# Forty more empty weight loads ahead of layer A's segments, and one more transposition ahead of the last outputs

## The chip, the cores and the metric

The kernel runs on one core of a Trainium2 chip. The metric is the device time of one execution in microseconds (us). The engines are named as in the profile: PE is TensorE's matrix multiplication and PEld its loading of weights, DVE is VectorE, ACT is ScalarE, POOL is GpSimd, SP is SyncE, which issues most of the DMA transfers.

## The reference

Four layers, A, B, A, B, each added to its input after a layer normalisation. Layer B is a linear attention and is not touched by the change. Layer A is recurrent: 2048 rows of 640 are cut into 64 segments of 32, and each segment is processed together with 8 memory rows that are the first outputs of the segment before.

```python
mem = mem0
for s in range(n_seg):                        # 64 segments of 32 rows
    xs = x[:, s * seg_len:(s + 1) * seg_len, :]
    h = jnp.concatenate([mem, xs], axis=1)    # 8 + 32 rows of 640
    q = jnp.einsum('btd,dhe->bhte', h, Wq)    # 32 heads of 192
    k = jnp.einsum('btd,dhe->bhte', h, Wk)
    v = jnp.einsum('btd,dhe->bhte', h, Wv)
    scores = jnp.einsum('bhqe,bhke->bhqk', q, k) * scale
    p = _softmax(jnp.where(mask[None, None], scores, -1000000000.0), axis=-1)
    o = jnp.einsum('bhqk,bhke->bhqe', p, v)
    o = jnp.einsum('bhte,hed->btd', o, Wo)
    mem = o[:, :M, :]                         # the next segment waits for this
    outs.append(o[:, M:, :])
```

## The kernel before

`A_pre` first does what does not depend on the memory: the keys, queries and values of the last 8 rows of every segment. `A_chain` then walks through the 64 segments in order. In it everything is in the order of the program text (`tc.manual_schedule()`): each engine executes its instructions in the order in which the Python code issues them, and semaphores make them wait for each other.

A segment has four rounds of eight heads. Per round TensorE projects queries, keys and values (`project`, line 1023, 20 matmuls each: five blocks of 128 input features in four column groups), computes scores (`scores`, lines 1060 and 1065), the sums of the exponentials (`sums`, line 1143, three matmuls), the weighted values (`attend`, line 1073, eight matmuls), and the round's share of the output product (`wo_round`, line 1102, 48 matmuls) into one PSUM tile `W` (`ps_w`). ACT and DVE turn one into the other: `normalise` takes logarithm and exponential of the sums on ACT (lines 1148 and 1149) and multiplies E on DVE (line 1150); `attend` ends with a copy of one half of OT on ACT (line 1079) and of the other on DVE (line 1080).

The end of a segment is the part that the change touches. There TensorE runs, in this order: the attention of round 2; `wo_round` of round 1, its last 24 matmuls around the three sums of round 3; 48 matmuls of `wo_round` of round 2 (whose OT lies in the tile `KT`); one matmul that only keeps TensorE busy (line 1109); `attend` of round 3; another such matmul; `wo_round` of round 3; four more busy matmuls (line 1116) and `fill(SEG_FILL)`, two weight loads of a single column (line 1122). DVE then transposes `W` (lines 1267 and 1268) into the first 8 columns of each 32-column block of `hT`, and the next segment's first projection waits for that.

The other columns of the next `hT` come from the next segment's rows, which have been loaded from DRAM long before (`load_rows`, POOL, line 974). `hx_transpose` (line 978) transposes them on DVE, in four instructions of 160 columns each. One of the four is issued between `normalise` of round 3 and the copies at the end of its `attend`; the other three come after these copies. `load_rows` for the segment after the next one is issued behind the fourth, since it overwrites the rows.

`fill(n)` issues n weight loads of one column, which compute nothing. `FILL` gives their number once per layer A, in its first segment, behind the first query projection:

```python
to_rows(q_or_k("Q", 0), "Q")
if s == 0:
    fill(FILL[li])
to_rows(q_or_k("K", 0), "K")
```

A segment has 510 matmuls, each with its weight load, and the two loads of `fill(SEG_FILL)`: 1022 TensorE instructions. The trace shows two semaphore instructions more on TensorE's queue in each segment, which makes 1024.

SP's queue carries the weights that don't fit into SBUF: per segment the slots of wQ, wK and wV (`load_slots`, line 694) near its beginning, and the output weights of the last round (`load_wo`, line 726, three transfers called wo_rows) near its middle. POOL's queue carries the small transfers: kqb (line 994), vb (line 1006), otb (line 1093).

Of the kernel before, what the change touches and what calls it, by code (L numbers as in the profile page):

```python
# [17 lines left out]
SLOTS = {"Q": 3, "K": 3, "V": 3}  # L18
LN_EPS = 1e-5

FILL = {0: 78, 2: 79}
SEG_FILL = 2

LATE = 64512
# [91 lines left out]
class Kernel:  # L116
# [834 lines left out]
    def A_chain(self, xn_dram, at_dram, li, load_slot, piece, load_wo, late_wo, wo_mid, wo_end, low, copy_slots):  # L951
# [3 lines left out]
        with tc.tile_pool(name=f"A{li}_ch", reuse_waits="tile", bufs=1) as sp, \  # L955
# [17 lines left out]
            def load_rows(s):  # L973
                nc.gpsimd.dma_start(out=xr[8:32, :], in_=xn_dram[32 * s:32 * s + 24, :])

            def hx_transpose(hT, gs):
                for g in gs:
                    nc.vector.transpose(out=hT[32 * g:32 * g + 32, :, :],
                                        in_=xr[:, 160 * g:160 * g + 160].rearrange("p (j b) -> p b j", b=KC))

            def new_hT():
                return sp.tile([P, KC, 32], BF16, name="hT", tag="hT")
# [53 lines left out]
            def to_rows(raw, m):  # L1036
                if m == "K":
                    nc.vector.transpose(out=KT[:, :, 0:64], in_=raw[:, :].rearrange("p (c j) -> p c j", j=64))  # L1038
                else:
                    rv = raw[:, :].rearrange("p (x i j) -> p x i j", i=3, j=64)  # L1040
                    nc.vector.transpose(out=QT[:, :, 0:4:3, 0:64], in_=rv[:, :, 0:3:2, :])  # L1041
                    nc.vector.transpose(out=QT[0:64, :, 1, 0:64], in_=rv[0:64, :, 1, :])
                    nc.vector.transpose(out=QT[64:P, :, 2, 0:64], in_=rv[64:P, :, 1, :])  # L1043
# [53 lines left out]
            def wo_round(W, r, OT, first, last, part=range(12)):  # L1097
                w = low[:, 0:7680] if last_wo == r else wo_end[:, :] if r in (0, 3) else wo_mid[:, 7680 * (r - 1):7680 * r]
                for i in part:
                    c, q = i % 6, 32 * (i // 6)  # L1100
                    for g in range(4):
                        nc.tensor.matmul(W[32 * g:32 * g + 32, 0:160], lhsT=OT[:, c, q:q + 32],  # L1102
                                         rhs=w[:, 640 * i + 160 * g:640 * i + 160 * g + 160], start=(first and i == 0),
                                         stop=(last and i == 11), tile_position=(0, 32 * g), skip_group_check=True)
# [14 lines left out]
            def fill(n):  # L1119

                for _ in range(n):
                    nc.tensor.ldweights(self.ident[:, 0:1])  # L1122
# [39 lines left out]
            hT = new_hT()  # L1162
# [3 lines left out]
            for s in range(NSEG):  # L1166
# [6 lines left out]
                def q_or_k(m, n):  # L1173
                    ps = pqp.tile([P, 512], F32, name="ps_qk", tag="qk")
                    project(hT, ps, m, n, s, range(KC))
                    return to_raw(ps, "OT" if m == "K" and n == 0 else "raw")
# [11 lines left out]
# [3 lines that stand above are left out]
# [54 lines left out]
                normalise(S, E)  # L1245
                if s + 1 < NSEG:
                    hT = new_hT()
                    hx_transpose(hT, range(1))
                wo_round(W, order[L - 1], OT, False, False)
                idle = pqp.tile([P, 512], F32, name="ps_idle", tag="qk")  # L1250
                keep_busy(idle, 1, 384)
# [2 lines left out]
                if s == NSEG - 1:  # L1254
                    self.first_tails = tails, [self.spread_tails(0, tails[0], low, "vvss")]
                if s + 1 < NSEG:
                    hx_transpose(hT, range(1, 4))
                    if s + 2 < NSEG:
                        load_rows(s + 2)
                keep_busy(idle, 1, 512)  # L1260
# [91 lines left out]
```

## Time and profile before

| | us |
|---|---|
| median of 3 runs | 3619.94 |
| the runs | 3619.16, 3619.94, 3630.49 |
| the profiled execution | 3620.12 |
| its span in the trace | 3618.4 |
| PE busy | 3296.9 (91%) |
| DVE busy | 2331.4 (64%) |
| ACT busy | 2028.7 (56%) |
| 64 segments of the first layer A | 204.3 to 1551.6 |
| 64 segments of the second | 2019.7 to 3367.0 |

A segment takes 1347.3 / 64 = 21.05 us on average, and the 128 of them are 74% of the span. The granted TensorE clock is 1.00 in both stretches, so the times of the trace need no correction for it. "Busy" of PE includes modelled ends of pipelined matmuls. In rows of waits, "issue" is time in which an engine waited for nothing that the profile shows.

### The profile page before, as it was taken

To read this page: it belongs to the slowest core of one execution; us is meant where nothing else is said; L and a number is where in the kernel's file an instruction comes from. 1 tells how busy PE (TensorE), PEld (TensorE's weight loads), DVE (VectorE), ACT (ScalarE), POOL (GpSimd) and SP (SyncE) were. 2 spreads that over 40 slices of the span, in tenths; PEclk is the share of its full clock that TensorE was granted. 3 is DMA by queue.
4 is the path that set the end of the run, shared out by engine and by line. 5 is a ranking of instruction groups with operands and counts; after the bars stand their busy time and mean duration, and the time that the engine had idled before them with its cause. 6 is when DMAs were issued, how large, how long until landed. Compare 5 with 4: busy or idle time off the path is not lost.

```text
span 3618.4 us, 166133 instructions
## 1 busy us (share of the span) xinstructions
PE 3296.9 (91%) x70978; PEld 2277.0 (63%) x71391; DVE 2331.4 (64%) x6320; ACT 2028.7 (56%) x5233; POOL 1596.8 (44%) x4173
## 2 busy tenths in 40 slices
PE   9989898998999989889999889899999899998999
PEld 7756666666666666655377566666666666666553
DVE  5456666766666766646633566666666666666465
ACT  3356565666566656546433556665666566665463
POOL 3445555555555555430123455555545555554400
PEclk9999999999999999999999999999999999999999
DMA  8888877777777777760476777777777777777600
GB/s 321 327 314 315 308 290 271 294 290 283 269 292 283 293 269 285 284 222 1 145 276 214 287 269 284 288 291 274 286 295 285 273 276 292 290 280 272 233 1 30
DMA packets 261055, 936.23 MB, mean 259 GB/s; under 512 B 53962, under 2 KB 104026, under 8 KB 226778
## 3 DMA queue, kind: packets, MB, share of 16 engines
q1 hardware_dynamic: 190650, 824.56, 60.0%
q0 software_dynamic: 67744, 87.80, 7.8%
q8 instruction: 557, 9.13, 1.0%
q10 hardware_dynamic: 1920, 13.24, 0.9%
q14 instruction: 184, 1.51, 0.1%
HBM read 855.58 MB, written 80.81 MB: 259 GB/s over the span
## 4 chain that ended last, share of the span: by engine, by line
PE 57%; DVE 12%; ACT 10%; issue 9%; DMA 6%; PEld 4%; POOL 1%; SPq 1%; ACTq 0%; DVEq 0%; POOLq 0%
PE ps_qk L1023 15%; PE ps_w L1102 9%; PE ps_v L1023 6%; PE ps_o L1073 5%; PE ps_pre L913 4%; PE ps_s L1065 4%; DVE E L1150 3%; ACT raw L1033 3%; DVE QT L1041 3%; ACT ps_s L1149 3%; PEld L1102 3%; ACT ps_s L1148 2%; DVE QT L1043 2%; PE ps_pre L937 2%; PE ps_s L1060 2%
## 5 line engine op out<-in xcount | busy, mean ns | idle before, releaser
L1023 PEld LDWEIGHTS <-hT 128*32 128x32 bf16 x30720 | 873.7, 96 | 435.5 <-DVE hT L1268 73.2
L1023 PE MATMUL ps_qk<-arena,hT 128*32 128x384 bf16 x20480 | 1043.0, 328 | 87.0 <-DVE hT L1268 75.1
L1033 ACT ACTIVATE raw<-ps_qk 128x384 bf16<-128x384 f32 x1024 | 502.9, 491 | 380.6 <-DVE QT L1043 251.9
L1023 PE MATMUL ps_v<-arena,hT 128*32 128x384 bf16 x10240 | 594.1, 326 | 9.0 <-DMA arena<-wV 5.4
L1006 POOL DMA_DIRECT2D Vp<-vb x512 | 259.2, 506 | 631.3 <-PE ps_o L1073 589.5
L1102 PE MATMUL ps_w<-arena,OT 128*32 128x160 bf16 x18432 | 466.8, 234 | 12.2 <-DMA arena<-wo_rows 4.8
L1102 PEld LDWEIGHTS <-OT 128*32 128x32 bf16 x18432 | 389.9, 97 | 75.4 <-ACT OT L1079 46.1
L1038 DVE STREAM_TRANSPOSE KT<-raw 128x384 bf16<-128x384 bf16 x512 | 296.2, 579 | 193.6 <-ACT raw L1033 189.7
L1041 DVE STREAM_TRANSPOSE QT<-raw 128x256 bf16<-128x256 bf16 x512 | 228.1, 445 | 239.6 <-ACT raw L1033 195.9
L994 POOL DMA_DIRECT2D kqb<-kqb x512 | 292.1, 571 | 169.1 <-POOL KT L1002 147.0
L1093 POOL DMA_DIRECT2D otb<-otb x512 | 283.9, 554 | 116.7 <-DVE otb L1089 88.6
L1054 DVE CAST Vp<-ps_v 64x384 bf16<-64x384 f32 x512 | 286.2, 559 | 69.6 <-ACT Vp L1052 57.4
L1150 DVE TENSOR_TENSOR E<-E,ps_s 80x320 bf16<-80x320 bf16 x512 | 247.1, 483 | 113.7 <-ACT ps_s L1149 113.3
L1073 PEld LDWEIGHTS <-Vp 80*128 80x128 bf16 x4096 | 200.5, 99 | 152.2 <-issue 137.6
L1052 ACT ACTIVATE Vp<-ps_v 64x384 bf16<-64x384 f32 x512 | 244.9, 478 | 90.2 <-PE ps_v L1023 90.1
L1073 PE MATMUL ps_o<-E,Vp 80*128 80x80 bf16 x4096 | 233.9, 202 | 62.9 <-DVE E L1150 43.2
L986 ACT ACTIVATE Vp<-ps_w 32x160 bf16<-32x160 f32 x512 | 150.7, 294 | 232.8 <-PE L1122 175.2
L1127 ACT ACTIVATE E<-ps_s 80x320 bf16<-80x320 f32 x512 | 221.8, 433 | 76.4 <-PE ps_s L1065 36.4
L1079 ACT ACTIVATE OT<-ps_o 128x192 bf16<-128x192 f32 x384 | 126.3, 329 | 246.0 <-PE ps_o L1073 230.8
L1102 PE MATMUL ps_w<-arena,KT 128*32 128x160 bf16 x6144 | 162.9, 238 | 106.4 <-issue 106.3
L1080 DVE CAST OT<-ps_o 128x192 bf16<-128x192 f32 x384 | 137.5, 358 | 161.6 <-PE ps_o L1073 152.0
L999 POOL COPY QT<-kqb 128x64 bf16<-128x64 bf16 x512 | 125.4, 245 | 251.4 <-PE ps_s L1065 247.7
(158 smaller groups left out, 5514.4 us busy)
## 6 DMA issues: line engine op xcount, KB each, us to landing
arena<-wK SPq DMA_DIRECT2D x121, 1152.0 KB, 7.7
arena<-wV SPq DMA_DIRECT2D x117, 1152.0 KB, 10.3
arena<-wo_rows SPq DMA_DIRECT2D x128, 960.0 KB, 6.2
arena<-wQ SPq DMA_DIRECT2D x125, 768.0 KB, 5.6
arena<-wo_rows SPq DMA_DIRECT2D x128, 640.0 KB, 7.8
arena<-wQ SPq DMA_DIRECT2D x125, 384.0 KB, 3.9
arena<-wo_rows SPq DMA_DIRECT2D x140, 320.0 KB, 8.1
arena<-in_A_Wv_dram SPq DMA_DIRECT2D x76, 384.0 KB, 8.6
```

The costliest lines, as they stand in the source:

```text
L994: nc.gpsimd.dma_start(out=kqb[:], in_=self.kqb_d[r, :, s, :])
L1006: nc.gpsimd.dma_start(out=Vs[n % 2][64:80, :], in_=self.vb_d[s, r].rearrange("g t f -> (g t) f"))
L1023: nc.tensor.matmul(o[32 * g:32 * g + 32, 0:384], lhsT=hT[:, b, :], rhs=rhs, start=(i == 0), stop=(i == KC - 1), tile_position=(0, 32 * g), ...
L1033: nc.scalar.activation(out=raw[:], in_=ps[:, 0:384], func=ACT.Copy)
L1038: nc.vector.transpose(out=KT[:, :, 0:64], in_=raw[:, :].rearrange("p (c j) -> p c j", j=64))
L1041: nc.vector.transpose(out=QT[:, :, 0:4:3, 0:64], in_=rv[:, :, 0:3:2, :])
L1052: nc.scalar.activation(out=o, in_=i, func=ACT.Copy)
L1054: nc.vector.tensor_copy(out=o, in_=i)
L1073: nc.tensor.matmul(O[x][:, 80 * i:80 * i + 80], lhsT=Vs[n % 2][0:80, 448 * x + k:448 * x + k + 128], rhs=E[0:80, 160 * x + 80 * e:160 * x ...
L1093: nc.gpsimd.dma_start(out=self.otb_d[:, s, 96 * r:96 * r + 96], in_=otb[:, :, :].rearrange("p c t -> p (c t)"))
L1102: nc.tensor.matmul(W[32 * g:32 * g + 32, 0:160], lhsT=OT[:, c, q:q + 32], rhs=w[:, 640 * i + 160 * g:640 * i + 160 * g + 160], start=(firs ...
L1150: nc.vector.tensor_tensor(out=E[0:80, 0:320], in0=E[0:80, 0:320], in1=rc, op=ALU.mult)
```

## The change

`FILL[0]` goes from 78 to 118: forty more one-column weight loads in the first segment of the first layer A. As TensorE has a single stream of instructions, everything behind them stands 40 places later in it, in that layer and in all that follow, the second layer A with its unchanged 79 included. And `hx_transpose` does two of its four transpositions, not one, between `normalise` of round 3 and the copies of `attend`; two are left behind these copies.

```diff
-FILL = {0: 78, 2: 79}
+FILL = {0: 118, 2: 79}
...
                 normalise(S, E)
                 if s + 1 < NSEG:
                     hT = new_hT()
-                    hx_transpose(hT, range(1))
+                    hx_transpose(hT, range(2))
                 wo_round(W, order[L - 1], OT, False, False)
                 idle = pqp.tile([P, 512], F32, name="ps_idle", tag="qk")
                 keep_busy(idle, 1, 384)
...
                 if s + 1 < NSEG:
-                    hx_transpose(hT, range(1, 4))
+                    hx_transpose(hT, range(2, 4))
                     if s + 2 < NSEG:
                         load_rows(s + 2)
                 keep_busy(idle, 1, 512)
```

The order of every engine's instructions is otherwise the same in both kernels.

## The prediction

> **What bounds the kernel now.** I read first the page's busy times, then the waits of PE, then the timeline of one ordinary segment's end, then the DMA view in narrow windows. The page:
>
> ```profile
> PE 3296.9 (91%) x70978; PEld 2277.0 (63%) x71391; DVE 2331.4 (64%) x6320; ACT 2028.7 (56%) x5233; POOL 1596.8 (44%) x4173
> ...
> q8 instruction: 557, 9.13, 1.0%
> ```
>
> PE is the bound on average, but look at the instruction queue: 557 packets, 9.13 MB, so 16.4 KB each. PE and PEld have 70978 + 71391 = 142369 instructions, 255.6 per packet: TensorE's program arrives in blocks of 256. A segment of 1024 instructions is four blocks exactly, so the borders fall on the same four places of every segment.
>
> The waits of PE (line waited for, us in total, times, longest):
>
> ```profile
> PE ps_w L1102 <- issue: 106.3, 119, 2.3
> PE ps_qk L1023 <- DVE hT L1268: 75.1, 126, 0.7
> PE ps_o L1073 <- DVE E L1150: 43.2, 129, 0.9
> ```
>
> The largest has no releaser: 119 times, 0.89 us each, nearly once per segment. The timeline of the segment that runs from 2659.66 to 2680.83 shows where (start, duration, engine, line):
>
> ```profile
> 2675.49 0.10 PEld L1143 LDWEIGHTS <-ones_blk 80*32 80x32 bf16 x3
> 2675.50 0.44 PEld L1102 LDWEIGHTS <-OT 128*32 128x32 bf16 x16
> ...
> 2675.90 0.10 PEld L1102 LDWEIGHTS <-KT 128*32 128x32 bf16 x1
> 2675.91 0.41 ACT L1148 ACTIVATE ps_s<-ps_s 80x320 f32<-80x320 f32 x1 [0.21 <-PE ps_s L1143]
> ...
> 2676.35 0.41 ACT L1149 ACTIVATE ps_s<-ps_s 80x320 f32<-80x320 f32 x1
> ...
> 2677.16 1.01 PE L1102 MATMUL ps_w<-arena,KT 128*32 128x160 bf16 x47 [0.95 <-issue]
> ...
> 2677.38 0.47 DVE L1150 TENSOR_TENSOR E<-E,ps_s 80x320 bf16<-80x320 bf16 x1
> ...
> 2678.27 0.45 PE L1073 MATMUL ps_o<-E,Vp 80*128 80x80 bf16 x8
> ...
> 2678.76 0.36 DVE L1080 CAST OT<-ps_o 128x192 bf16<-128x192 f32 x1 [0.53 <-PE ps_o L1073]
> ...
> 2679.00 1.01 PE L1102 MATMUL ps_w<-arena,OT 128*32 128x160 bf16 x48
> ...
> 2679.15 1.10 DVE L978 STREAM_TRANSPOSE hT<-Vp 32x160 bf16<-32x160 bf16 x3
> ...
> 2680.29 0.28 DVE L1267 STREAM_TRANSPOSE wt<-ps_w 128x96 f32<-128x96 f32 x1
> ```
>
> The first KT matmul runs at once, the other 47 of the same group wait until 2677.16: a block border, with the next block not there. Meanwhile ACT and DVE do the normalisation, whose sums went out just before. The DMA view shows the segment's four instruction packets begin near 2660.87, 2668.38, 2674.84 and 2678.26. The third is the block that PE waits for; from its start to PE's restart are 2.32 us.
>
> **The border, 40 places earlier.** Counting back from the second KT pair: one KT pair, 16 OT pairs, 3 sum pairs, 20 pairs, 40 instructions. The new border lies exactly ahead of the three sums. PE reaches it at 2675.49; call the time at which the block is there R. The wait now delays the sums, so normalisation comes after it and not beside it. From the first sum's weights to the end of the multiplication: ACT ends at 2676.76, DVE adds 0.03 + 0.47, so 2677.26 - 2675.49 = R + 1.77 (here the multiplication came later, 2677.38, behind two otb copies). PE needs less for the 64 matmuls between (0.41 + 0.94) and the busy one (0.17), R + 1.52, so `attend` waits for E: R + 1.81.
>
> **The transposition moved** (344 to 393 ns each in the row of line 978) is worth something where it was: the three end at 2680.25, 0.04 before line 1267, while PE's last `wo_round` is over at 2679.00 + 1.01 = 2680.01. One fewer there would give 0.24. But ahead of the copy it has room only while E is early (multiplication over at 2677.85, copy at 2678.76). With `attend` right behind E, two transpositions end at +0.76 after the multiplication, the outputs are ready at +0.52, so the copy waits 0.25: starts at +0.78, ends at +1.14; from its end to line 1267 goes by PE, 2680.01 - 2679.12 + 0.03 = 0.92. Line 1267 starts at R + 1.77 + 2.06 = R + 3.83. Before it was 2680.29: break-even is R = 2676.46. POOL's `load_rows` stays behind the fourth transposition.
>
> **R.** The third fetch follows the entry into the block before. The old border there is 128 pairs ahead of the KT one, reached near 2670.75; the new one is 20 pairs of line 1023 earlier, 0.81 us, 2669.94. Bounds: the delay to the packet stays (4.1 us), R = 2677.16 - 0.81 = 2676.35, 0.11 gained; the packet starts when it did, R = 2677.16, 0.70 lost. What decides is the DMA traffic, and POOL's transfers show how it treats a request (KB, us from issue to landing; issued at 2665.12, 2667.53, 2669.31, 2669.88, 2671.88):
>
> ```profile
> kqb<-kqb POOLq DMA_DIRECT2D x1, 48.0 KB, 6.8
> ...
> Vp<-vb POOLq DMA_DIRECT2D x1, 28.0 KB, 5.5
> ...
> kqb<-kqb POOLq DMA_DIRECT2D x1, 48.0 KB, 5.3
> ...
> otb<-otb POOLq DMA_DIRECT2D x1, 24.0 KB, 7.2
> ...
> Vp<-vb POOLq DMA_DIRECT2D x1, 28.0 KB, 5.7
> ```
>
> They land at 2671.9, 2673.0, 2674.6, 2677.1, 2677.6. The first two: issued 2.41 apart, landed 1.1 apart, 0.46 us per us. The last two: 2.0 apart, landed 0.5 apart; behind SP's wo_rows (issued 2669.20 to 2670.48) asking earlier brings little. The second fetch is also just in time: 2668.38 + 2.32 = 2670.70 against PE at 2670.75. Asked 0.81 earlier it comes 0.37 earlier by the first slope, so PE stands 0.44 at the second border, and the third request is 0.37 early, not 0.81. With an unchanged delay from there, R = 2677.16 - 0.37 = 2676.79, which I take: it lies between the bounds and nearer to neither. Cost: 2676.79 + 3.83 - 2680.29 = 0.33 us per segment. The stand at the second border costs nothing of its own, being shorter than the wait that follows.
>
> The fourth fetch follows R, the border it serves lies in the last busy matmuls, and PE waits 0.60 for hT there: covered. The forty weight loads: 78 took 1.01 us at the first segment, so 0.52 once. In layer B and `A_pre` the waits of PE show no such entry: nothing.
>
> **Sum** against the profiled execution, 3620.12 us (0.18 from the median): 126 x 0.33 + 0.5 = 42, so 3662, rounded to 3660. About 0.3%, 11 us, is what a measurement here can tell from no change.
>
> [...]
>
> **Rivals.**
> - The borders' places don't matter, only the transposition does: the wait keeps its effect and 0.24 x 126 = 30 us are gained, 3590. Against it: what the wait covers changes. 0.06.
> - The third fetch gets ahead of the wo_rows traffic: with the second fetch's delay (2665.98 to 2668.38, 2.4) it starts at 2672.3, the block is there before 2675.49, and E bounds: multiplication over at 2677.85 (otb copies), line 1267 at 2679.91, 0.38 gained, more where otb is early. Partly so, R = 2676.1, 0.36. Some 45 to 75 us, 3575 to 3545. For it: 2669.94 lies before SP's last wo_rows issue. 0.20.
> - R within 0.09 of break-even, no change: 3620. 0.12.
> - The packet keeps its place behind wo_rows: 0.70 x 126 = 88, 3708. For it: otb, issued 2669.88, lands with those issued 2 us later. 0.20.
> - My forecast, R from 2676.55 to 2677.0: 11 to 70 us slower. 0.42.
>
> **Numbers.** Faster 0.06 + 0.20, same 0.12, slower 0.42 + 0.20. The range reaches from 3575, which leaves out the farther half of the fast case, to 3715, past the full loss. The forecast's own range is 3631 to 3690.
>
> **What would show it.** Right: the PE wait on "issue" leaves line 1102 and stands ahead of line 1143, ending near 1.3 us; PE line 1073 waits longer for line 1150; line 1080 starts some 0.25 after its outputs; 3 becomes 2 in the last row of line 978; a wait in a projection near 2669.9 of this segment. Wrong: no wait ahead of line 1143, the third instruction packet more than 1.2 us earlier in its segment, or a time under 3609.

## The result, and the profile after

| | before | after |
|---|---|---|
| median, us | 3619.55 (4 runs, 3615.25 to 3630.49) | 3709.04 (4 runs, 3701.61 to 3717.83) |
| profiled execution, us | 3620.12 | 3701.61 |
| ratio | | 1.0243, interval 1.0212 to 1.0275 |

The change costs 89 us. The direction and most of the mechanism are those of the forecast; the amount is near that of the rival "the packet keeps its place behind wo_rows" (3708), though not from its sum alone, as the last part of the account shows.

The page of the changed kernel:

```profile
PE 3369.9 (91%) x70978; PEld 2269.3 (61%) x71431; DVE 2334.3 (63%) x6320; ACT 2030.6 (55%) x5233; POOL 1590.2 (43%) x4173
...
q8 instruction: 557, 9.13, 1.0%
```

There are 40 more weight loads (71431 against 71391), as many instruction packets, and no more work on DVE and ACT. PE's 73 us more of "busy" come with the same 70978 matmuls: their ends are modelled, and it is no more work. The waits of PE (line waited for, us in total, times, longest):

```profile
PE ps_s L1143 <- issue: 60.2, 43, 2.0
PE ps_s L1143 <- ACT KT L1079: 50.1, 74, 1.1
PE ps_o L1073 <- DVE E L1150: 42.8, 129, 0.7
PE ps_qk L1023 <- DVE hT L1268: 31.6, 100, 0.4
PE ps_v L1023 <- issue: 22.7, 47, 1.0
PE ps_v L1023 <- DMA arena<-wV: 14.8, 16, 5.3
PE ps_idle L1116 <- issue: 13.0, 13, 2.8
```

The largest entry of before, 106.3 us at line 1102, is gone. In its place stand 60.2 + 50.1 = 110.3 us ahead of the sums of line 1143. The second of the two names ACT, whose copy to KT had ended 1.1 us before the wait was over (below), so it is read as the block border as well. Of the 43 + 74 waits, 59 lie in the first layer A and 58 in the second: the forty loads of the first moved the border in both. "PE ps_v L1023 <- issue" is new: the stand at the second border.

The timeline of an ordinary segment of the second layer A, from 3273.65 to 3295.54 (start, duration, engine, line):

```profile
3284.38 0.77 PEld L1023 LDWEIGHTS <-hT 128*32 128x32 bf16 x22 [0.41 <-issue]
...
3289.71 0.33 ACT L1079 ACTIVATE KT<-ps_o 128x192 bf16<-128x192 f32 x1
...
3291.11 0.10 PEld L1143 LDWEIGHTS <-ones_blk 80*32 80x32 bf16 x3 [1.25 <-issue]
...
3291.47 0.41 ACT L1148 ACTIVATE ps_s<-ps_s 80x320 f32<-80x320 f32 x1 [1.44 <-PE ps_s L1143]
...
3291.91 0.41 ACT L1149 ACTIVATE ps_s<-ps_s 80x320 f32<-80x320 f32 x1
3292.35 0.48 DVE L1150 TENSOR_TENSOR E<-E,ps_s 80x320 bf16<-80x320 bf16 x1 [1.04 <-ACT ps_s L1149]
...
3292.86 0.71 DVE L978 STREAM_TRANSPOSE hT<-Vp 32x160 bf16<-32x160 bf16 x2
3292.89 0.45 PE L1073 MATMUL ps_o<-E,Vp 80*128 80x80 bf16 x8
...
3293.61 0.36 DVE L1080 CAST OT<-ps_o 128x192 bf16<-128x192 f32 x1
...
3294.88 0.28 DVE L1267 STREAM_TRANSPOSE wt<-ps_w 128x96 f32<-128x96 f32 x1
```

Read it from the row of 3291.11: PE has stood 1.25 us and sends the first weights of the sums when the block is there. ACT has waited 1.44 us for the sums, DVE 1.04 for ACT. Before, this time lay beside the normalisation; now the normalisation comes after it. `attend` starts as soon as E is multiplied (3292.83), and the copy of line 1080 stands behind two transpositions, 0.72 after `attend` starts and not 0.49.

Where single segments scatter, medians tell more. All medians below are over the 126 ordinary segments of a run (all but the first of each layer A), worked out from the trace's records, in us from a segment's first instruction. The borders follow from counting off 256 instructions: a segment has 1024, and in the median four packets start in it, before and after. "Needed" is when PE's last instruction ahead of the border starts, "there" when the first one behind it does.

| | before | after |
|---|---|---|
| second block needed, there | 11.19, 11.28 | 10.38, 10.73 |
| third packet starts | 15.12 | 15.02 |
| third block needed, there (R) | 16.42, 17.54 | 16.18, 17.45 |
| multiplication over (L1150) | 17.88 | 19.18 |
| `attend` starts (L1073) | 18.66 | 19.24 |
| line 1267 starts | 20.68 | 21.28 |

PE gets to the third border 0.24 earlier and is let through 0.09 earlier, yet E is ready 1.30 later. Some of that was slack: before, `attend` came 0.78 after E. So line 1267 is 0.60 later, 126 x 0.60 = 76 us. PE's wait for wV was this before:

```profile
PE ps_v L1023 <- DMA arena<-wV: 5.4, 2, 4.6
```

It is 14.8 now, 9 more, and the 118 empty loads take 1.84 us where the 78 took 1.01, 0.8 more: 86, where the profiled executions differ by 81.5.

### The profile page after: what moved, and what is told of

It reads as the page before. It is cut to its first block, busy times and chain, and to the rows that moved or that the text cites. A ratio compares the mean times of both kernels' runs of the same rounds, so it can differ in the third digit from the quotient of the medians.

```text
span 3699.9 us, 166173 instructions
## 1 busy us (share of the span) xinstructions
PE 3369.9 (91%) x70978; PEld 2269.3 (61%) x71431; DVE 2334.3 (63%) x6320; ACT 2030.6 (55%) x5233; POOL 1590.2 (43%) x4173
## 3 DMA queue, kind: packets, MB, share of 16 engines
q10 hardware_dynamic: 1920, 13.24, 0.9%
## 4 chain that ended last, share of the span: by engine, by line
PE 54%; DMA 12%; DVE 12%; ACT 11%; issue 9%; PEld 1%; POOL 1%; SPq 1%; ACTq 0%; DVEq 0%; POOLq 0%
PE ps_qk L1023 14%; PE ps_w L1102 8%; PE ps_v L1023 7%; DMA arena<-wV 6%; PE ps_o L1073 5%; PE ps_pre L913 4%; DVE E L1150 4%; ACT ps_s L1149 3%; PE ps_s L1065 3%; ACT ps_s L1148 3%; ACT raw L1033 3%; DVE QT L1041 2%; PE ps_pre L937 2%; PE ps_s L1060 2%; DVE QT L1043 2%
## 5 line engine op out<-in xcount | busy, mean ns | idle before, releaser
L1023 PEld LDWEIGHTS <-hT 128*32 128x32 bf16 x30720 | 861.1, 97 | 446.4 <-issue 93.9
L1023 PE MATMUL ps_qk<-arena,hT 128*32 128x384 bf16 x20480 | 1031.8, 328 | 40.7 <-DVE hT L1268 31.6
L1023 PE MATMUL ps_v<-arena,hT 128*32 128x384 bf16 x10240 | 626.0, 327 | 44.1 <-issue 22.7
L1102 PE MATMUL ps_w<-arena,OT 128*32 128x160 bf16 x18432 | 508.8, 235 | 14.4 <-DMA arena<-wo_rows 5.1
L1150 DVE TENSOR_TENSOR E<-E,ps_s 80x320 bf16<-80x320 bf16 x512 | 247.3, 483 | 212.9 <-ACT ps_s L1149 212.6
L1073 PEld LDWEIGHTS <-Vp 80*128 80x128 bf16 x4096 | 199.4, 99 | 186.5 <-issue 178.5
L1148 ACT ACTIVATE ps_s<-ps_s 80x320 f32<-80x320 f32 x512 | 214.7, 419 | 157.5 <-PE ps_s L1143 157.5
L1073 PE MATMUL ps_o<-E,Vp 80*128 80x80 bf16 x4096 | 233.8, 202 | 69.6 <-DVE E L1150 42.8
L1143 PE MATMUL ps_s<-E,ones_blk 80*32 80x320 bf16 (+1 forms) x1536 | 159.5, 305 | 110.3 <-issue 60.2
L1065 PE MATMUL ps_s<-QT,KT 128*80 128x80 bf16 (+1 forms) x3072 | 233.1, 213 | 2.0 <-POOL KT L1002 1.8
```

The lines of the kernel that those rows point to most:

```text
L1023: nc.tensor.matmul(o[32 * g:32 * g + 32, 0:384], lhsT=hT[:, b, :], rhs=rhs, start=(i == 0), stop=(i == KC - 1), tile_position=(0, 32 * g), ...
L1065: nc.tensor.matmul(S[0:80, c0:c0 + 80 * (q1 - q0)], lhsT=KT[:, 3 * x + i, :], rhs=QT[:, x, q0:q1, :], start=False, stop=(x == 1 and i == 2 ...
L1073: nc.tensor.matmul(O[x][:, 80 * i:80 * i + 80], lhsT=Vs[n % 2][0:80, 448 * x + k:448 * x + k + 128], rhs=E[0:80, 160 * x + 80 * e:160 * x ...
L1148: nc.scalar.activation(out=rc, in_=rc, func=ACT.Ln)
L1150: nc.vector.tensor_tensor(out=E[0:80, 0:320], in0=E[0:80, 0:320], in1=rc, op=ALU.mult)
```

## The experiments

Ratios are against the kernel before on the same chip.

**One part at a time.** First the border alone:

```diff
-FILL = {0: 78, 2: 79}
+FILL = {0: 118, 2: 79}
```

> Only the forty weight loads, one transposition ahead of the copies as before. Theory (the block border ahead of the sums, its block arriving when the wo_rows traffic lets it, makes the whole loss): with `attend` right behind the multiplication the copy isn't held up, but three transpositions follow it, which gives R + 3.82 for line 1267 against R + 3.83 with two; so 3709 us within 6, and the wait ahead of line 1143 as in the changed kernel. Rival (the second transposition holds up the copy and that is a good part of the loss): under 3690.

Measured: 3727.21 us (3717.47 to 3752.52), ratio 1.0285, 1.0229 to 1.034. That is 3723 us by the 3619.55 of before, above the 3709 within 6 that was expected. Then the transposition alone:

```diff
-                    hx_transpose(hT, range(1))
+                    hx_transpose(hT, range(2))
...
-                    hx_transpose(hT, range(1, 4))
+                    hx_transpose(hT, range(2, 4))
```

> Only the second transposition moved, the borders where they were. Theory: where the border stands behind the sums, the multiplication is over 0.9 us before the copy, so two transpositions have room, and the end of the chain on DVE comes 0.24 us earlier in 126 segments: 3620 - 30 = 3590 us. Rival (the moved transposition delays the copy of OT in any case, or PE's last product is the later one): 3620 or above.

Measured: 3604.94 us (3595.78 to 3606.54), ratio 0.9939, 0.9909 to 0.9968, some 22 us of the 30 that were expected. The waits of PE with the border alone, then with the transposition alone:

```profile
PE ps_s L1143 <- issue: 66.9, 49, 2.2
PE ps_s L1143 <- ACT KT L1079: 45.9, 70, 1.2
```

```profile
PE ps_w L1102 <- issue: 108.2, 121, 2.0
PE ps_qk L1023 <- DVE hT L1268: 48.5, 126, 0.4
```

The border alone makes the wait at line 1143 (112.8 us) and the whole loss, by the ratios a little more, though the two intervals overlap. The transposition alone gains 0.6%: line 1267 starts at 20.51 and not 20.68, 0.17 x 126 = 21 us, and PE's wait for `hT` falls from 75.1 to 48.5. The two ratios multiply to 1.0222, within the interval of both together.

**Is it the border's place, or the moved fetches?** The changed kernel with the borders six places later than it has them, just behind the three sums:

```diff
-FILL = {0: 118, 2: 79}
+FILL = {0: 112, 2: 79}
```

> The changed kernel with 34 places instead of 40: the border stands right behind the three sums instead of right ahead of them, everything else alike. Theory: the third block arrives at the same time, 17.44 us after the segment's begin, but the normalisation now runs beside the wait; PE needs 0.34 + 0.94 + 0.17 us from there to `attend`, 18.9 against 18.65 before, and the transposition gives 0.24 back: 3625 us, within 15, and a wait in PE line 1102 in place of that in line 1143. Rival (what counts is how early the third block is asked for, not where the wait stands among the instructions): 3700, as the changed kernel.

Measured: 3632.56 us (3622.2 to 3646.6), ratio 1.0021, 1.0003 to 1.0039. The waits of PE:

```profile
PE ps_w L1102 <- issue: 105.2, 120, 2.5
```

The second block is late as in the changed kernel (needed at 10.40, there at 10.91), the third is there at 17.52, and the wait is as long as before, 105.2 us. But the three sums are out ahead of it, and 2.2% of the time is back. So the loss is what stands behind the border when PE waits, not the wait.

**What holds the third packet.** The changed kernel without the reload of wo_rows:

```diff
-                                load_wo(order[L])
```

> The changed kernel without the reload of the last round's output weights (no wo_rows transfers in the middle of a segment but the last; the products use the weights of another round). Theory (the third instruction packet is held up by this traffic): the packet starts 2 us or more before its 15.0 us after the segment's begin, the wait ahead of line 1143 is gone, and the multiplication sets the end: 0.4 to 1.0 us less than the kernel before per segment, 3500 to 3570 us. Rival (the delay of 4 us or so belongs to the fetch itself): the packet starts where it did, the wait stays, 3690 or more.

Measured: 3574.45 us (3565.96 to 3578.76), ratio 0.9849, 0.9821 to 0.9878. And without the reload of wK and wV, wo_rows kept:

```diff
         def load_slots(m, r, b):
+            if m in "KV":
+                return
```

> The changed kernel without the reload of the weight slots of K and V in each segment (the output is therefore not the reference's); wo_rows is loaded as before. It asks what keeps the third packet back. Theory (wo_rows do): the second block comes in time, TensorE doesn't stand at the second border, yet the third packet still starts at 14 us of its segment or later, and TensorE still waits ahead of line 1143; the time is 3660 to 3710, ratio 1.01 to 1.025. Rival (the lateness is inherited from the transfers of wK and wV, which push wo_rows back): the third packet starts at 13 or earlier, no wait ahead of line 1143, ratio 0.975 to 0.99.

Measured: 3499.96 us (3497.0 to 3503.02), ratio 0.966, 0.9644 to 0.9677. The waits of PE without wo_rows, then without wK and wV (its line 1145 is 1143 of the others):

```profile
PE ps_v L1023 <- issue: 44.6, 101, 1.2
```

```profile
PE ps_s L1145 <- issue: 4.2, 3, 1.7
```

Either load taken away frees the third packet: it starts at 12.35 without wo_rows, at 11.28 without wK and wV, and in the median PE doesn't stand at the third border in either. Here the theory of the second of these runs (wo_rows alone hold it) fell: 1.92 MB of wo_rows do not hold the packet when 2.3 MB are not queued ahead of them. With both loaded it starts at 15.02.

**Borders still earlier, and later.** 80 places earlier than before, at the scores of round 3, and 40 places later than before, inside the KT pairs:

```diff
-FILL = {0: 118, 2: 79}
+FILL = {0: 158, 2: 79}
```

> The changed kernel with the borders another 40 places earlier (80 earlier than before), at the beginning of the scores of round 3. Theory (the third packet starts near 15.0 us of a segment, 2.4 us ahead of TensorE's restart, whenever it is asked for in these microseconds): TensorE stands from about 15.8 until 17.4, and the scores, the exponentials and the sums all come behind that: 1.2 to 1.8 us more per segment than before, 3770 to 3850, ratio 1.04 to 1.065. Rival (asked for early enough the packet gets ahead of wo_rows): it starts at 13.9 or earlier, TensorE waits less than 0.6 there, and the time is 3660 or less, ratio below 1.01.

```diff
-FILL = {0: 78, 2: 79}
+FILL = {0: 38, 2: 79}
```

> The kernel before with FILL[0] of 38 and not 78: the borders stand 40 places later, the third 20 pairs behind the first KT pair, in the middle of line 1102's 48. Theory (the block is there at a fixed time, or with 0.3 us of delay per us that it is asked for later): TensorE does 0.41 us of work ahead of the border that it did behind it; the request is 0.7 later and the block 0 to 0.2 later, so line 1267 starts 0.2 to 0.4 earlier: 25 to 52 us less, 3568 to 3595, ratio 0.986 to 0.993. Rival (the delay from request to packet is fixed, as the lower bound of the prediction had it): the block is 0.7 later, line 1267 0.3 later, 3655, ratio 1.01.

Measured: 80 earlier 3680.94 us (3672.32 to 3685.83), ratio 1.0157, 1.0135 to 1.018; 40 later 3761.77 us (3748.86 to 3767.14), ratio 1.0374, 1.0344 to 1.0404. The waits of PE, 80 earlier and then 40 later:

```profile
PE ps_s L1065 <- issue: 109.7, 110, 1.9
PE ps_w L1102 <- issue: 48.4, 78, 2.4
```

```profile
PE ps_w L1102 <- issue: 176.0, 126, 2.5
PE ps_qk L1023 <- issue: 76.5, 122, 1.7
```

Both expectations missed. 80 earlier, the second block is entered at 10.10, and the third packet starts at 14.11, 0.9 us before that of the changed kernel; R is 16.50 and PE stands 1.23. That is neither the theory's 15.0 nor the rival's 13.9. The second row, 48.4 us, is the fourth border, which now lies in the last round's product. 40 later, every border moves, the first past the attention of round 0: it is entered at 7.94 and not at 6.19, so the packet of the second block starts at 10.82 and PE stands 0.99 at the second border, where the theory had it standing nowhere. PE's entry into the second block, taken for the request of the third (below), is then at 13.27 and not 12.0, the packet starts at 16.47, R is 19.08. I had costed the border that I looked at and not the three others.

**Less behind the block.** The kernel before, with 32 of the 48 pairs of round 2's product moved behind the attention of round 3 (the second busy matmul cut to 64 columns):

```diff
-                wo_round(W, order[L - 1], OT, False, False)
+                wo_round(W, order[L - 1], OT, False, False, range(4))
+                OT2 = OT
...
+                wo_round(W, order[L - 1], OT2, False, False, range(4, 12))
...
-                keep_busy(idle, 1, 512)
+                keep_busy(idle, 1, 64)
```

> The kernel before, with the last 32 of the 48 matmuls of the output product of round 2 moved behind the attention of round 3. Theory (the third instruction block is there at about 17.5 us of a segment whatever TensorE does, and what counts is the work that still stands between that time and the attention): E is ready at 17.9 and the attention starts 0.1 behind it, at about 18.0 and not at 18.7; the moved matmuls run beside the copies of the attention's outputs, and line 1267 starts at about 20.0 and not at 20.7. 0.6 us x 126 = some 80 us less, about 3540, ratio 0.975 to 0.985. Rival (the end of a segment is set by DVE's transpositions or by weights that land late, not by what stands behind the block): 3600 or more, ratio above 0.993.

Measured: 3602.52 us (3590.08 to 3613.62), ratio 0.9947, 0.9927 to 0.9968. R is 17.60, `attend` starts at 18.19, the copies end at 19.03 and the transpositions at 20.17: all earlier, as wanted. But line 1267 (1269 in this kernel) starts at 20.44, only 0.24 earlier, since from 18.57 on PE works without a pause through 80 pairs until 20.4. From R to there are 2.8 us, and PE is at work for nearly all of them, whatever their order. The expectation counted the wait and not that work; the time is in the rival's range, but for this reason and not for the two that the rival names.

**Moving the traffic.** The kernel before, with the last 960 of wo_rows' 1920 KB issued on SP behind a store that waits for round 1's tail:

```diff
-                    if n > 0:
+                    if n == 2 and s < NSEG - 1:
+                        store_tail(otb, s, order[n - 1], nc.sync)
+                        load_wo(order[L], cuts=((3, 5), (5, 6)))
+                    elif n > 0:
                         store_tail(otb, s, order[n - 1])
...
-                                load_wo(order[L])
+                                load_wo(order[L], cuts=((0, 3),))
```

(`cuts` says which sixths of the 1920 KB to load; `load_wo` and `store_tail` got an argument for this, not shown.)

> The kernel before, with the second and third transfer of wo_rows (960 of 1920 KB) issued on SP's queue behind the store of round 1's tail and so near 13 us of a segment and not at 10.0 and 10.4; that one store goes over SP and not POOL. Theory (the third packet waits for the weights that are queued ahead of it when it is asked for, at 11.3): 960 KB less at some 0.37 MB per us, less than 2.7 us of delay and not 3.8, so it starts before 14.0, the block is there before TensorE gets to the border at 16.4, the wait at line 1102 is gone, the attention starts near 17.9 and not 18.7, line 1267 0.4 to 0.7 earlier: 50 to 90 us less, 3530 to 3570, ratio 0.975 to 0.986. Rival (the delay does not depend on what is queued, or the late weights are missing at the last wo_round): 3600 or more, ratio 0.995 or above.

Measured: 3643.64 us (3624.2 to 3666.21), ratio 1.0053, 1.0026 to 1.0079. The same split in the changed kernel:

> The changed kernel with the same split of wo_rows and the borders left where the change puts them. Theory (the place of the border costs only because the block is late there): the third packet starts before 13.9, TensorE doesn't stand ahead of line 1143, the stand at the second border (0.35) stays: 3540 to 3600, ratio 0.977 to 0.994, within 30 us of the split with the borders of before. Rival (the place itself costs, or the packet stays at 15.0): 3660 or more, ratio above 1.01.

Measured: 3773.02 us (3754.96 to 3784.61), ratio 1.0398, 1.0354 to 1.0442. All three transfers late, in the kernel before:

> As the split, with all three transfers of wo_rows behind that store, near 13 us. Theory: the third packet starts near 12.4, as without wo_rows, and TensorE doesn't stand at line 1102; but the weights land near 19.2, about when the last wo_round wants them (19.4), and the fourth packet, asked for at 16.4, is the one that now waits behind them. Between 3540 and 3640, ratio 0.978 to 1.005, not better than the split. Rival (landing late is no matter): below 3530, ratio under 0.975.

Measured: 4150.92 us (4143.23 to 4156.55), ratio 1.1444, 1.1409 to 1.1479. The waits of PE with the split, with the split in the changed kernel, and with all three late:

```profile
PE ps_w L1102 <- DMA arena<-wo_rows: 58.2, 133, 1.7
...
PE ps_qk L1023 <- issue: 46.8, 66, 1.6
...
PE ps_w L1102 <- issue: 12.2, 19, 1.5
```

```profile
PE ps_idle L1116 <- issue: 67.0, 80, 3.0
PE ps_s L1143 <- issue: 49.3, 33, 2.7
```

```profile
PE ps_w L1102 <- DMA arena<-wo_rows: 443.7, 315, 3.0
```

All three missed: the two splits landed in the range of their rivals, and with all three transfers late the time lies far above the range, away from its rival. The split does what it was for: the third packet starts at 14.11, and the wait at line 1102 falls from 106.3 to 12.2 us. But the store that holds the late part goes out later than I had put it, at 14.7 and not 13, so PE waits 58.2 us for wo_rows; and the second packet starts at 9.30 and not 8.84, 46.8 us at the second border. In the changed kernel, with weights issued late, the fourth packet is later too (it starts at 19.59 and not 18.74, 67.0 us at line 1116), and the third starts at 14.80 only. With all three late the third packet comes 1.17 us after its request (12.63 to 13.81) and PE doesn't stand for it, but it stands 443.7 us for the weights. A smaller portion, the last 320 KB alone, with two transpositions:

> The kernel before with two transpositions ahead of the last outputs, and with the last 320 KB of wo_rows (the part that the last wo_round reads last) behind the store of round 1's tail, near 14.7 us of a segment. Theory (the third packet waits for what is queued ahead of it): it starts at 14.2 to 14.6 and not at 15.1, the block is there 0.5 to 0.9 earlier, line 1267 0.3 to 0.6 earlier than with the two transpositions alone, the 320 KB land by 18.5 and nobody waits for them: 3530 to 3570, ratio 0.974 to 0.985. Rival (the late piece or the store on SP costs as much as the earlier block brings): 3605 or more, ratio 0.993 or above.

Measured: 3605.36 us (3602.79 to 3608.42), ratio 0.9956, 0.994 to 0.9973: the rival's case, and what the transposition gives by itself. The third packet starts at 15.18, as if nothing had been moved. Waits of PE:

```profile
PE ps_w L1102 <- issue: 105.6, 122, 2.0
```

**The third packet in all runs.** "Asked for" is PE's entry into the second block. That the request goes out there is a reading of the traces, not a record in them: in the ordinary segments of all 14 runs exactly one packet starts between PE's entry into one block and its entry into the next, for the second and the third block alike, and never less than 0.20 us behind the first of the two. By then SP had issued these parts of wo_rows (960, 640 and 320 KB, in most runs at 9.54, 9.95 and 10.43). "Moved" is what SP's queue moved between the request and the packet's start, counted from the trace's DMA records:

| run | asked for | wo_rows issued by then, KB | starts | delay | moved, KB |
|---|---|---|---|---|---|
| all three late | 12.63 | 0 | 13.81 | 1.2 | 30 |
| no reload of wo_rows | 10.98 | 0 | 12.35 | 1.4 | 90 |
| no reload of wK, wV | 10.23 | 1600 | 11.28 | 1.1 | 140 |
| 80 places | 10.10 | 1600 | 14.11 | 4.0 | 1330 |
| split | 11.75 | 960 | 14.11 | 2.4 | 770 |
| split, changed kernel | 10.90 | 960 | 14.80 | 3.9 | 1230 |
| after | 10.73 | 1920 | 15.02 | 4.3 | 1350 |
| border behind the sums | 10.91 | 1920 | 15.04 | 4.1 | 1420 |
| border alone | 10.95 | 1920 | 15.16 | 4.2 | 1360 |
| before | 11.28 | 1920 | 15.12 | 3.8 | 1360 |
| transposition alone | 11.28 | 1920 | 15.23 | 4.0 | 1360 |
| less behind the block | 11.37 | 1920 | 15.24 | 3.9 | 1330 |
| last 320 KB late | 11.28 | 1600 | 15.18 | 3.9 | 1340 |
| 40 later | 13.27 | 1920 | 16.47 | 3.2 | 1120 |

Asked for anywhere between 10.7 and 11.4, with the first 1600 KB out, the packet starts between 15.0 and 15.2. In the split the weights' queue falls from 293 to 102 KB per us at 14, just when the packet starts; in the 40-later kernel it falls from 376 to 197 at 16, and the packet starts at 16.47. That looks like a step, the end of a transfer, and not a slope in the time of the request. But other rows speak against a step. With 1600 KB issued, the packet asked for at 10.10 starts at 14.11 and the one asked for at 11.28 starts at 15.18: the delay is the same. And with 960 KB issued, the one asked for at 10.90 starts later than the one asked for at 11.75.

What stays nearest to one value is the last column. Nine of the runs load wK and wV and had 1600 or 1920 KB of wo_rows issued by the request. In eight of them the queue moved 1330 to 1420 KB before the packet started, whenever it was asked for (10.10 to 11.37), while the delay goes from 3.8 to 4.3 us; in the ninth, 40 later, it moved 1120 KB in 3.2 us, and its rate had fallen before the packet started. So in these eight the delay is better told in weights, 7% from the least to the most, than in microseconds, 13%. That is a count; it shows no mechanism. In the changed kernel the median segment's 1350 KB took 4.15 us, 0.33 MB per us, and before 1360 KB took 3.81, 0.36 MB per us. The weights are also further behind there: 4 us into a segment the queue has moved 540 KB, and 840 before. That came with the border, as it is 504 with the border alone and 822 with the transposition alone, and it fits the longer waits for wV. Why the weights start later, and move more slowly, no run here shows. That 320 KB fewer at the end of the queue brought nothing (15.18) fits: 1340 KB had moved by then as well.

What also stays open is how the order comes about. Without wK and wV, wo_rows had been issued 0.7 and 0.3 us ahead of the request, and the packet started with 140 KB moved; 80 places earlier, with nearly the same lead, it started with 1330 KB moved. No run here shows the queue itself.

## Why the prediction was off in size

Point by point, in the order of its steps.

- **Blocks of 256 and the border exactly ahead of the sums**: right. The wait left line 1102 and stands at line 1143. One of its signs failed: PE's wait at line 1073 for line 1150 was to grow, and it is 42.8 us against 43.2. In the segment above the matmul of line 1109 lasts until 3292.80, by its modelled end, and `attend` starts at 3292.89, so little is left to wait.
- **The second border**: PE was to stand 0.44 there and the block to come 0.37 earlier. Measured: it stands 0.35 and the packet starts 0.45 earlier (8.39 against 8.84). Right, within 0.1.
- **R to line 1267, 3.83 us**: 21.28 - 17.45 = 3.83. Right, with its parts: multiplication at R + 1.73 (1.77), line 1267 another 2.05 later than that in the median of the segments (2.06).
- **The copy behind two transpositions, 0.25**: 0.72 against 0.49 after `attend` starts, 0.23. Right. That it makes the transposition worthless at this border is borne out too: with the border alone line 1267 starts 2.07 after the multiplication, with both 2.05; what the pair gains over the border alone (1.0243 against 1.0285) is not clear of the noise, as the two intervals overlap.
- **The transposition where the border was, 0.24**: 0.17. Right in the main, and a third less.
- **The fourth fetch is covered**: in the median the block is 0.24 late (needed at 21.04, there at 21.28), but that falls into PE's wait for `hT`, which drops from 75.1 to 31.6 us; 13.0 us stand at line 1116.
- **The size of R**: this is the step that failed. In the segment that the prediction used, R = 2676.79 is 17.13 in the segment; the median measured is 17.45. Forecast was a loss of 0.33 per segment, measured is 0.60 (that segment reached line 1267 0.05 earlier than the median one). The missing 0.27 x 126 = 34 us and the 9 of wV lead from 3662 to 3705, where the profiled execution has 3701.6.

R was taken as R of before less 0.37, on the argument that the request is 0.37 earlier and the delay stays. The step that failed is the unchanged delay: the request was 0.55 earlier (10.73 against 11.28), the packet only 0.10, and R 0.09, so the delay grew from 3.8 to 4.3 us. What stayed was the amount that the weights' queue moved meanwhile, 1360 and 1350 KB, but it moved at 0.36 MB per us before and at 0.33 after; why is open. The prediction took the traffic as it was before. A view at hand pointed that way: the prediction itself read that otb, asked for 0.6 ahead of the last wo_rows, landed with transfers asked for 2 us later, and wrote that behind wo_rows "asking earlier brings little". It then took the middle of the bounds because the value was near neither end.

That the measured time falls on the rival's 3708 is in part luck. That rival has 0.70 lost per segment, 88 us; measured are 0.60, 76 us, and only the 9 us of wV, which were not forecast, bring the sum to 86.

## What to carry to other kernels

When an engine's largest wait has no releaser and recurs at the same instruction of a loop, count its instructions against the blocks in which its program is fetched (256 here); then ask what stands just behind the border: 110.3 us of waits ahead of the sums went with a ratio of 1.0243, 105.2 behind them with 1.0021. Six places, from ahead of three small matmuls to behind them, were worth 2.2% here. Moving one border moved them all here (40 places later, the first is passed at 7.94 and not 6.19, the second at 13.27 and not 11.28), so cost each of them, with the work between it and the last. And don't carry a fetch's delay over in microseconds: in eight runs here it was nearest to a fixed amount of weights moved, 1.33 to 1.42 MB, so ask how that traffic will run in the changed kernel.

Of the versions run here that load all their weights, three are a little faster than the kernel before: two transpositions ahead of the copies at the old border (ratio 0.9939, 0.9909 to 0.9968), the same with the last 320 KB of wo_rows late (0.9956, 0.994 to 0.9973), and 32 pairs behind the attention (0.9947, 0.9927 to 0.9968).

## What of the hardware was not expected

- An instruction block's fetch, from the request as read above to the packet, took 1.1 to 1.4 us where the weights' queue moved 30 to 140 KB meanwhile, and 3.8 to 4.3 where it moved 1330 to 1420 KB. From the packet to TensorE's going on are another 2.34 to 2.61 (between the medians given above, at the borders where it stood).
- Neither half of the traffic holds it alone: without 1.92 MB of wo_rows, or without 2.3 MB of wK and wV, the third packet starts at 12.35 or 11.28 and not 15.02, and PE's stand there goes from 1.1 us a segment to nothing.
- A transfer of 320 KB more or less among those issued last moved the fetch by nothing measurable (15.18 against 15.12 and 15.23).
